# Attention and two feed-forwards on one core: the feed-forwards without GpSimd, weights in order of deadline

## The chip, the cores and the metric

The kernel runs on one core of a Trainium2 chip. The metric is the device time of one execution in microseconds (us); lower is better. Engines are called TensorE (PE in the rows, its weight loads PEld), VectorE (DVE), ScalarE (ACT), GpSimd (POOL) and SyncE (SP, which issues all DMAs here).

## The reference

```python
def reference(q, k, v, moe_*, moe2_*):             # q, k, v: (4, 8, 576, 64)
    x = attention(rotate(q), rotate(k), v)           # softmax(q k^T / 8) v
    x = x.transpose(0, 2, 1, 3).reshape(2304, 512)
    h = x @ moe_w_in                                 # 512 x 2048
    g = np.where(h > 0, h, np.exp(np.minimum(h, 0)) - 1)
    x = g @ moe_w_out                                # 2048 x 512
    a, b = x @ moe2_w1, x @ moe2_w2                  # 512 x 1024 each
    return (a * b @ moe2_w3) @ moe2_w_out            # 1024 x 1024, 1024 x 512
```

All values are float32.

## The kernel before, in words

Every large product is made from two-part operands: a value is split into a high part (a copy rounded to the type that the matmul reads) and a rest (value minus high part, also rounded), and three matmuls (high by high, high by rest, rest by high, `PAIRS` of line 24) stand for one. A split is one copy (`copy_hi`, lines 81 to 87) and one subtraction (line 79). Operations on whole tiles are mostly 128 partitions by 512 columns.

**Weights.** They come from memory as 64-bit words (`fetch_w`, line 92). `weight_steps` (line 97) turns one 128x512 block into its two parts in six steps: `rebase` (ScalarE, line 110), `shift`, `low` and `sign` (VectorE, lines 113, 116, 119), `high` (ScalarE, line 124) and `rest` (line 128, on the engine handed in: GpSimd).

**Stage 1**, attention, runs to about 304 us. It also prepares the first six blocks of w_in and of w_out (`PF` = 6). It is not changed.

**Stage 2**, the first feed-forward (lines 535 to 695). Five token tiles, three of 512 and two of 384 columns (`TT`), by 16 blocks f of the hidden width make 80 steps, numbered n. `part_h` (line 566) does 12 matmuls for h; then relu and exp on ScalarE, e on VectorE (line 577), and g's split: the copy on ScalarE (line 83), the rest on VectorE (line 79). `part_y` (line 582) does 12 matmuls of g with w_out into four banks that collect over f. The list `behind` holds y back by `LAG` = 2 steps; g has `LAG` + 1 buffers. When a tile ends, all y that are still held back are done before the next tile's first h, and the next tile's x is split (`split_x`, line 548).

Blocks of weights become due in `todo_w` (line 666): w_in and w_out alternate by f, one and a half a step, the last at step 13. `ready_in_out` issues the first four steps behind the h of one step and leaves `high` and `rest` in the list `late`, which the next `part_h` empties between exp and e. From step 15 on, `EARLY` (line 49) names the steps in which the second feed-forward's weights are made: 24 blocks of w_out2 and w3 (`ready_early`, 4/3 a step over steps 15 to 32) are split, stored in memory (`keep`) and later read back (`again`); then 16 blocks of w1 and w2 (`ready_half`), of which each pair is combined on GpSimd into seven blocks of 256 columns, split on GpSimd and stored. A staging tile has two buffers and a raw block has two. In the last token tile w_out2 (`load_o`) and w3 (`load_3`) are read back into the slots of w_in and w_out whose last reader is done; these DMAs stand in SyncE's queue and wait there.

**Stage 3**, the second feed-forward (lines 698 to 871). First W = w3 w_out2 is made, 24 matmuls for each of eight blocks (`part_w`, line 711); between blocks the x of the first token pair is summed (`x_sums`, line 728, on GpSimd) and split (`x_split`). Then come 24 groups (`group`, line 816): seven products of 384 columns (`multiply`, line 769) from which VectorE and ScalarE make two gates (`gate`), and, one group later, 18 matmuls of the gates with W (`part_o`, line 786). When eight groups are done, six outputs are copied out of their banks into a buffer of four (`ev`) and stored.

Each engine works through its instructions in their order. In stage 2 that order is written out by hand, step by step:

```python
part_h(ti, f, x[ti])
behind.append((ti, f))
if len(behind) > LAG:
    part_y(*behind.pop(0))
while todo_w and todo_w[0][0] <= n:
    ...
```

Of the kernel before, what the change touches and what calls it, by code (L numbers as in the profile page):

```python
# [18 lines left out]
P = 128  # L19
# [27 lines left out]
NA = 2 * PF  # L47

EARLY = (*(15 + 3 * i // 4 for i in range(24)), *(n for f in range(8) for n in (33 + 5 * f, 34 + 5 * f)))

LOAD_O = (0, 1, 1, 2, 3, 3, 4, 5)
LAG, LOAD_3, DEEP, W_AT = 2, 6, 2, NA
# [8 lines left out]
def kernel(  # L61
# [468 lines left out]
    def load_3(i):  # L530
        for z in range(2):
            w3_t[i, z] = slot(8 + 2 * (i % DEEP) + z, F32R, [P, 2, 512], "w")
            again(w3_t[i, z], ("3", i, z))

    with ExitStack() as c2:
# [5 lines left out]
        g_p = pool2("g", LAG + 1)  # L541
# [22 lines left out]
        gs, ys, late = {}, {}, []  # L564

        def part_h(ti, f, x):
# [52 lines left out]
        halves = {}  # L619

        def ready_half(key):
# [11 lines left out]
            pool.tensor_tensor(t1, b12, b11, op=ALU.subtract)  # L633
            pool.tensor_tensor(t2, b22, t1, op=ALU.subtract)
            pool.tensor_tensor(b12, b22, b12, op=ALU.subtract)
            order = (b11, b21, t2, t1, b12, b21, b22)
            for y in range(0, 7, 2):
                blocks = order[y:y + 2]
                st = stage_p.tile([P, len(blocks), 2, 256], F32R, tag="stage", name="wab", padded_shape=[P, 2, 2, 256])
                for i, b in enumerate(blocks):  # L640
                    if y + i == 5:
                        pool.tensor_tensor(b, b, t2, op=ALU.subtract)
                    copy_hi(st[:, i, 0], b, pool)
                    pool.tensor_tensor(st[:, i, 1], b, st[:, i, 0].bitcast(F32), op=ALU.subtract)
                keep(("ab", f, y // 2), st)
# [15 lines left out]
        for i in range(DEEP):  # L661
# [271 lines left out]
```

## Time and profile before

| | |
|---|---|
| median of three runs | 1047.61 us (1044.87 to 1047.69) |
| the profiled execution | 1042.17 us, its span 1040.4 us |
| TensorE busy | 1011.4 us, 97% |
| VectorE busy | 626.8 us, 60% |
| ScalarE busy | 497.2 us, 48% |
| GpSimd busy | 424.8 us, 41% |
| VectorE by slices of 26 us, stage 2 | about 8 of 10 up to 490 us, about 5 of 10 after |
| granted TensorE clock, mean | 0.994 |

A row of the trace names the line, the engine, the operation and the tiles (result<-operands). "Busy" of TensorE holds matmuls whose ends are modelled, so a short wait may not show as a gap; how many matmuls a stretch holds shows it. An idle time in brackets is followed by what ended it.

### The profile page before, as it was taken

What the parts mean: (1) busy time and instruction counts of PE and PEld (TensorE: products, weight loads), DVE (VectorE), ACT (ScalarE), POOL (GpSimd) and SP (SyncE); (2) the same over time, 40 slices, a digit from 0 to 9 for tenths busy, and PEclk for the clock granted to TensorE, in tenths of its full rate; (3) what the DMA queues carried; (4) which work ended last, traced back from release to release, by engine and by line L of the source; (5) the groups of instructions that cost most, each with busy time, mean ns of one, the idle gap of its engine ahead of it and who ended that gap; (6) DMA issues with size and microseconds to landing.
All of it is one profiled execution on the core that took longest, in us unless ns stands there. A gap on an engine that the chain in (4) does not pass through costs nothing.

```text
span 1040.4 us, 15562 instructions
## 1 busy us (share of the span) xinstructions
PE 1011.4 (97%) x5660; PEld 862.8 (83%) x5660; DVE 626.8 (60%) x1006; ACT 497.2 (48%) x1012; POOL 424.8 (41%) x465
## 2 busy tenths in 40 slices
PE   8999999999999989998999999999999999999997
PEld 7777777777768768876888999999899899999996
DVE  5698989888748888787534555532333444434323
ACT  3677777777645656555533444443223232222222
POOL 3789888888303332322544365560500211300000
PEclk9999999999999999999999999999999999999999
DMA  5988787876661005677332233466464446555511
GB/s 175 255 232 243 220 241 217 241 220 184 205 257 68 1 1 175 249 242 244 122 124 102 93 148 139 188 240 223 162 218 159 160 164 215 158 162 209 172 66 61
DMA packets 63101, 180.86 MB, mean 174 GB/s; under 512 B 7984, under 2 KB 9648, under 8 KB 63024
## 3 DMA queue, kind: packets, MB, share of 16 engines
q1 hardware_dynamic: 63024, 179.86, 53.2%
q8 instruction: 45, 0.74, 0.3%
q14 instruction: 32, 0.26, 0.1%
HBM read 121.31 MB, written 31.98 MB: 147 GB/s over the span
## 4 chain that ended last, share of the span: by engine, by line
PE 66%; issue 12%; DVE 11%; ACT 4%; POOL 3%; DMA 3%; SPq 0%; ACTq 0%; POOLq 0%; DVEq 0%
PE h L561 11%; PE y L589 11%; PE A L774 9%; PE o L800 9%; PE B L774 7%; PE w L716 4%; POOL w L128 3%; PE o L402 3%; PE s L286 3%; DVE nm L298 3%; PE ptp L334 3%; DMA kept<-w 2%; PE s L278 2%; DVE wr L116 2%; ACT pr L302 1%
## 5 line engine op out<-in xcount | busy, mean ns | idle before, releaser
L589 PE MATMUL y<-g,w 128*128 128x512 f32 (+1 forms) x960 | 213.3, 371 | 8.0 <-ACT g L83 4.0
L561 PE MATMUL h<-xt,w 128*128 128x512 f32 (+1 forms) x960 | 211.7, 369 | 5.4 <-ACT w L124 2.6
L589 PEld LDWEIGHTS y<-g,w 128*128 128x128 f32 x960 | 175.4, 189 | 35.2 <-DVE g L79 7.6
L561 PEld LDWEIGHTS h<-xt,w 128*128 128x128 f32 x960 | 174.2, 188 | 32.3 <-ACT w L124 3.4
L302 ACT ACTIVATE pr<-s,nm 128x576 f32<-128x576 f32 x144 | 106.6, 740 | 61.3 <-DVE nm L298 60.1
L128 POOL TENSOR_TENSOR w<-wr,w 128x512 fp32r<-128x512 f32 x56 | 74.2, 1330 | 147.2 <-ACT w L124 126.5
L298 DVE TENSOR_REDUCE nm<-s 128x1 f32<-128x576 f32 x144 | 107.0, 750 | 19.9 <-PE s L278 13.1
L774 PE MATMUL A<-xc,set 128*128 128x384 f32 x576 | 116.1, 336 | 0.9 <-ACT p L826 0.8
L79 DVE TENSOR_TENSOR g<-e,g 128x512 fp32r<-128x512 f32 (+1 forms) x80 | 81.4, 1018 | 58.4 <-ACT g L83 48.6
L800 PE MATMUL o<-W,g 128*128 128x512 f32 x432 | 111.6, 394 | 0.4 <-DVE g L784 0.2
L774 PEld LDWEIGHTS A<-xc,set 128*128 128x128 f32 x576 | 102.4, 188 | 8.6 <-ACT p L826 2.2
L577 DVE SCALAR_TENSOR_TENSOR e<-e,h 128x512 f32<-128x512 f32 (+1 forms) x80 | 50.4, 630 | 74.7 <-ACT e L573 74.7
L286 PE MATMUL s<-st 128*128 128x288 f32 x480 | 93.1, 316 | 1.6 <-ACT pr L302 1.4
L800 PEld LDWEIGHTS o<-W,g 128*128 128x128 f32 x432 | 79.9, 188 | 13.7 <-DVE g L784 0.7
L334 PE MATMUL ptp<-idt,pr 128*128 128x128 f32 x576 | 91.0, 281 | 0.0
L83 ACT ACTIVATE g<-p 128x384 fp32r<-128x384 f32 x48 | 25.2, 526 | 134.3 <-DVE p L846 96.0
L334 PEld LDWEIGHTS ptp<-idt,pr 128*128 128x128 f32 x576 | 65.9, 143 | 27.8 <-issue 12.6
L774 PE MATMUL B<-xc,set 128*128 128x384 f32 x432 | 86.5, 334 | 0.0
L182 POOL TENSOR_TENSOR raw_qk<-raw_qk,tab 128x640 f32<-128x640 f32 (+1 forms) x56 | 83.2, 1486 | 2.2
L838 DVE TENSOR_TENSOR p<-A,p 128x384 f32<-128x384 f32 x24 | 13.4, 558 | 110.5 <-PE A L774 110.5
L572 ACT ACTIVATE e<-h 128x512 f32<-128x512 f32 (+1 forms) x80 | 43.8, 547 | 73.0 <-PE h L561 71.0
L774 PEld LDWEIGHTS B<-xc,set 128*128 128x128 f32 x432 | 76.0, 188 | 0.0
(323 smaller groups left out, 1480.9 us busy)
## 6 DMA issues: line engine op xcount, KB each, us to landing
set<-kept SPq DMA_DIRECT2D x72, 512.0 KB, 3.8
st<-hl SPq DMA_DIRECT2D x180, 144.0 KB, 2.5
raw<-w_ SPq DMA_DIRECT2D x32, 512.0 KB, 3.8
kept<-w SPq DMA_DIRECT2D x24, 512.0 KB, 3.3
kept<-wab SPq DMA_DIRECT2D x24, 512.0 KB, 2.6
w<-kept SPq DMA_DIRECT2D x24, 512.0 KB, 4.2
raw_qk<-k_ SPq DMA_DIRECT2D x15, 640.0 KB, 4.3
raw_qk<-q_ SPq DMA_DIRECT2D x15, 576.0 KB, 4.3
```

The costliest lines, as they stand in the source:

```text
L79: lo_eng.tensor_tensor(lo, src, hi.bitcast(F32), op=ALU.subtract)
L128: rest_eng.tensor_tensor(made[0][:, 1], r, made[0][:, 0].bitcast(F32), op=ALU.subtract)
L182: pool.tensor_tensor(r[:, z], r[:, z], tab[:, w, z, TAB[w]], op=ALU.mult)
L286: pe.matmul(s[:, n, :288], st[:, j, 0, c * P:c * P + P], st[:, j, z, n * 288:(n + 1) * 288], start=(z == 1), stop=(z == 2),)
L298: dve.tensor_reduce(nm, s[:, :, :288], axis=AX.XY, op=ALU.max, negate=True)
L302: act.activation(pr_t[u, c][:, j].rearrange("p (n i) -> p n i", n=2), s[:, :, :288], ACTF.Exp, bias=nm, accum_out=sums_t[u, hf][:, at_:at_ ...
L334: pe.transpose(pt[:, kc], pr[:, at_:at_ + P], idt)
L561: pe.matmul(ps[:, :n], w[:, a, cc * P:(cc + 1) * P], x[cc][:, c], start=(i == 0), stop=(i == 11))
L577: dve.scalar_tensor_tensor(g, e, -1.0, ps[:, :n], op0=ALU.add, op1=ALU.max)
L589: pe.matmul(ys[ti][o][:, :n], wout[f][:, a, o * P:(o + 1) * P], g[:, c], start=(f == 0 and i == 0), stop=(f == NF - 1 and i == 2),)
L774: pe.matmul(ps[:, :HB], w[:, a, c * P:(c + 1) * P], x[:, c, b], start=(start and i == 0), stop=i == 5, skip_group_check=True,)
L800: pe.matmul(outs[p, o], g[:, a, o % 3 * P:o % 3 * P + P], wW[f][:, c], start=(f == 0 and i == 0), stop=(f == NG - 1 and i == 2),)
```

## The change

- The rests of all weights (line 128) in the first feed-forward, the combining and splitting of w1 and w2, and the sums of x in the second, go from GpSimd to VectorE. The copies in the splits of w1 and w2 go to ScalarE.
- What a weight leaves for the next step is held in two lists. ScalarE's part (`late_act`) is issued after exp as before, VectorE's (`late_dve`) between e and g's rest.
- The seven blocks of a pair of w1 and w2 are made in four parts, one a step (`ready_part`).
- Weights of the first feed-forward are fetched and made in the order of the step that first reads them, 4/3 a step from step 0. The early weights are made one a step from step 17, and none in the first or the last step of a tile.
- `LAG` is 3; g keeps three buffers.
- Five blocks of w3 are read back in the last token tile (before: two), and the loads of the first two sets come between the blocks of W. x is summed and split ahead of each block of W.
- In a group the sums of x for the next pair follow the first add. In the last group the product that feeds the first gate comes before the one that feeds the second, and the last 18 matmuls run in order of their output.

```diff
-EARLY = (*(15 + 3 * i // 4 for i in range(24)), *(n for f in range(8) for n in (33 + 5 * f, 34 + 5 * f)))
+STEP = [n for n in range(17, 80) if n % 16 not in (15, 0)]
+EARLY = (*STEP[:24], *(n for f in range(8) for n in STEP[23 + 4 * f:25 + 4 * f]))
-LAG, LOAD_3, DEEP, W_AT = 2, 6, 2, NA
+LAG, LOAD_3, SLOT_3, W_AT = 3, (6, 7, 11, 12, 13), (8, 10, 14, 16, 18, 8, 10, 8), NA
...
-            w3_t[i, z] = slot(8 + 2 * (i % DEEP) + z, F32R, [P, 2, 512], "w")
+            w3_t[i, z] = slot(SLOT_3[i] + z, F32R, [P, 2, 512], "w")
...
-        g_p = pool2("g", LAG + 1)
+        g_p = pool2("g", 3)
...
             act.activation(e, e, ACTF.Exp, scale=-1.0)
-            while late:
-                late.pop(0)()
+            run(late_act)
             g = e
             dve.scalar_tensor_tensor(g, e, -1.0, ps[:, :n], op0=ALU.add, op1=ALU.max)
+            run(late_dve)
             t = g_p.tile([P, 2, n], F32R, tag="g", name="g", padded_shape=[P, 2, 512])
             split(t, g, act, dve)
...
-            steps = weight_steps(i, raws.pop(i), lambda t: (win, wout)[i % 2].__setitem__(i // 2, t), pool)
+            steps = weight_steps(i, raws.pop(i), lambda t: (win, wout)[i % 2].__setitem__(i // 2, t), dve)
             for step in steps[:4]:
                 step()
-            late.extend(steps[4:])
+            late_act.append(steps[4])
+            late_dve.append(steps[5])
...
-            steps = weight_steps(None, raws.pop(key), lambda t: done.__setitem__(0, t), pool)
+            steps = weight_steps(None, raws.pop(key), lambda t: done.__setitem__(0, t), dve)
...
-            late.extend((*steps[4:], lambda: keep(key, done[0])))
+            late_act.append(steps[4])
+            late_dve.extend((steps[5], lambda: keep(key, done[0])))
...
+        def ready_part():
+
+            if not parts:
+                return
+            f, y, blocks = parts.pop(0)
+            made = []
+            if y == 2:
+                dve.tensor_tensor(blocks[1], blocks[1], t2_of[f], op=ALU.subtract)
+
+            def high():
+                made.append(stage_p.tile(
+                    [P, len(blocks), 2, 256], F32R, tag="stage", name="wab", padded_shape=[P, 2, 2, 256]
+                ))
                 for i, b in enumerate(blocks):
+                    copy_hi(made[0][:, i, 0], b, act)
+
+            def rest():
+                for i, b in enumerate(blocks):
+                    dve.tensor_tensor(made[0][:, i, 1], b, made[0][:, i, 0].bitcast(F32), op=ALU.subtract)
+                keep(("ab", f, y), made[0])
+
+            late_act.append(high)
+            late_dve.append(rest)
...
-        todo_w = [(1 + 2 * w // 3, NA + w) for w in range(2 * NF - NA)]
+        todo_w = sorted(range(NA, 2 * NF), key=lambda i: (i // 2 + LAG * (i % 2), i))
+        fetch = list(todo_w)
+        todo_w = [(3 * w // 4, i) for w, i in enumerate(todo_w)]
...
+            last = n + 1 == N3
+            if last:
+                c12()
+                lows = g0(), c22()
+                for low in lows:
+                    low()
+                return
...
             for i in range(7):
-                part_w(i)
-                if i + DEEP < 8:
-                    load_3(i + DEEP)
+                if i in (2, 4):
+                    load_set(i // 2 - 1)
                 x_sums(0, i)
                 x_split(0, i)
+                part_w(i)
+                if i in (0, 1, 5):
+                    load_3({0: 5, 1: 6, 5: 7}[i])
...
-            part_o(N3 - 1, (3, 4, 5, 0, 1, 2))
+            part_o(N3 - 1, range(6))
```

## Rows read from the trace of the kernel before

**Rows 1.** Chain of waits in order of time: start us, us, what.

```profile
500.04 2.72 PE y L589 x12
...
707.71 6.24 PE y L589 x36
```

**Rows 2.** Timeline of TensorE: start us, us, instructions merged [idle before <-releaser].

```profile
304.42 2.11 PE L561 MATMUL h<-xt,w 128*128 128x512 f32 x8
...
308.01 0.49 PE L589 MATMUL y<-g,w 128*128 128x512 f32 x1 [1.48 <-ACT g L83]
...
382.83 0.73 PE L561 MATMUL h<-xt,w 128*128 128x512 f32 x2 [2.10 <-ACT w L124]
...
485.81 0.49 PE L589 MATMUL y<-g,w 128*128 128x512 f32 x1 [2.27 <-ACT g L83]
```

**Rows 3.** Busy us by stretches of 20 us; (x) counts instructions, PEclk is granted clock.

```profile
core 0: us, PE busy (x) PEld busy (x) DVE busy (x) ACT busy (x) POOL busy (x), PEclk, DMA share, GB/s
...
320.00:340.00 20.00, 20.00 (x90) 16.58 (x89) 16.97 (x23) 12.26 (x22) 7.27 (x6) 1.00 0.00 0
...
360.00:380.00 20.00, 18.01 (x76) 13.56 (x75) 16.90 (x22) 12.14 (x21) 7.95 (x6) 1.00 0.00 0
380.00:400.00 20.00, 17.08 (x73) 13.10 (x72) 15.23 (x24) 11.32 (x21) 2.75 (x2) 1.00 0.17 54
...
480.00:500.00 20.00, 15.81 (x60) 12.40 (x61) 14.75 (x23) 11.65 (x20) 4.08 (x4) 0.91 0.57 203
...
640.00:660.00 20.00, 19.23 (x106) 18.01 (x105) 14.16 (x21) 10.73 (x22) 10.98 (x16) 1.00 0.32 116
660.00:680.00 20.00, 20.00 (x118) 20.00 (x117) 10.52 (x16) 8.23 (x17) 12.17 (x16) 1.00 0.75 293
```

**Rows 4.** VectorE by line and shape, 310 to 385 us: count | busy us, mean ns | idle before.

```profile
L119 DVE SCALAR_TENSOR_TENSOR wr<-raw,wr 128x512 int32<-128x512 int32 x20 | 20.6, 1032 | 0.7
L79 DVE TENSOR_TENSOR g<-e,g 128x512 fp32r<-128x512 f32 x13 | 16.2, 1244 | 9.1 <-ACT g L83 9.1
L116 DVE SCALAR_TENSOR_TENSOR wr<-raw,wr 128x512 int32<-128x512 int32 x20 | 13.9, 693 | 0.7
L577 DVE SCALAR_TENSOR_TENSOR e<-e,h 128x512 f32<-128x512 f32 x13 | 8.8, 677 | 0.0
L113 DVE TENSOR_SCALAR wr<-wr 128x512 int32<-128x512 int32 x20 | 8.3, 416 | 0.0
```

**Rows 5.** Timeline of VectorE and GpSimd between 366 and 392 us.

```profile
371.71 1.67 DVE L119 SCALAR_TENSOR_TENSOR wr<-raw,wr 128x512 int32<-128x512 int32 x1
...
389.65 0.69 DVE L79 TENSOR_TENSOR g<-e,g 128x512 fp32r<-128x512 f32 x1 [0.70 <-PE y L589]
...
371.36 1.47 POOL L128 TENSOR_TENSOR w<-wr,w 128x512 fp32r<-128x512 f32 x1 [3.09 <-ACT w L124]
```

**Rows 6.** Timeline of ScalarE at the end of the second token tile.

```profile
473.74 0.63 ACT L124 ACTIVATE w<-wr 128x512 fp32r<-128x512 f32 x1 [3.05 <-DMA kept<-w]
...
481.83 0.68 ACT L110 ACTIVATE wr<-raw 128x512 f32<-128x512 f32 x1 [1.92 <-DMA raw<-w_]
```

**Rows 7.** Waits (who <- whom: us in total, times, longest) and VectorE's timeline, stage 3.

```profile
DVE p L838 <- PE A L774: 110.5, 24, 6.8
...
PE A L774 <- ACT p L826: 0.8, 2, 0.4
...
812.45 1.36 DVE L851 TENSOR_TENSOR p<-u,p 128x384 f32<-128x384 f32 x1
```

**Rows 8.** Timeline of TensorE and ScalarE at the end of the program.

```profile
1030.55 0.72 PE L800 MATMUL o<-W,g 128*128 128x512 f32 x2 [0.16 <-ACT g L83]
1031.50 3.92 PE L800 MATMUL o<-W,g 128*128 128x512 f32 x16 [0.23 <-DVE g L784]
...
1036.52 0.60 ACT L809 ACTIVATE ev<-o 128x512 f32<-128x512 f32 x1 [1.82 <-DMA out_<-ev]
```

**Rows 9.** SyncE's own waits; and DMA issues (count, KB each, us to landing).

```profile
SPq L524 <- PE h L561: 11.9, 1, 11.9
...
raw<-w_ SPq DMA_DIRECT2D x32, 512.0 KB, 3.8
```

More of the change, by code (lines that the diff above doesn't have):

```diff
@@ L562, in project, with run @@
                     i += 1
-        gs, ys, late = {}, {}, []
+        gs, ys, late_act, late_dve = {}, {}, [], []
+        def run(late):
+            while late:
+                late.pop(0)()
         def part_h(ti, f, x):
@@ L632, in ready_half @@
             t1, t2 = t[:, :256], t[:, 256:]
[L633 to L639, printed above, removed]
-                for i, b in enumerate(blocks):
[L641 to L645, printed above, removed]
+            dve.tensor_tensor(t1, b12, b11, op=ALU.subtract)
+            dve.tensor_tensor(t2, b22, t1, op=ALU.subtract)
+            dve.tensor_tensor(b12, b22, b12, op=ALU.subtract)
+            parts.extend((f, y, blocks) for y, blocks in enumerate(((b11, b21), (t2, t1), (b12, b21), (b22,))))
+            t2_of[f] = t2
+        def ready_part():
[9 more added lines that the diff above has]
+                ))
+                for i, b in enumerate(blocks):
+                    copy_hi(made[0][:, i, 0], b, act)
[5 more added lines that the diff above has]
+            late_dve.append(rest)
         ahead = [(ready_early, ("o", j, 0), w_o2[j]) for j in range(8)]
@@ L692 @@
                     task(i)
+            run(late_act)
+            run(late_dve)
             for s_ in behind:
                 part_y(*s_)
-        assert not ahead and not tasks
+        assert not ahead and not tasks and not parts
     with ExitStack() as c3:
@@ L821, in group @@
             more = p + 1 < NPAIR
-            if more and f and f != 6:
-                x_sums(p + 1, {7: 6}.get(f, f - 1))
             multiply(A, x[0], w[0], True)
@@ L828, in group @@
             dve.tensor_tensor(p1, B_[:, :HB], p1, op=ALU.add)
+            if more and f and f != 6:
+                x_sums(p + 1, {7: 6}.get(f, f - 1))
             part_o(n - 1, (3, 4))
@@ L843, in group, with c22, c12, g0 @@
                 x_split(p + 1, {7: 6}.get(f, f - 1))
[L844 to L852 removed]
+            def c22():
+                multiply(A, x[5], w[5], False)
+                if last:
+                    part_o(n - 1, (1, 2))
+                dve.tensor_tensor(p5, A[:, :HB], p5, op=ALU.mult)
+                return gate(n, 1, p5)
+            def c12():
+                multiply(B_, x[6], w[6], False)
+                dve.tensor_tensor(u2, B_[:, :HB], u2, op=ALU.add)
+            def g0():
+                dve.tensor_tensor(p1, u2, p1, op=ALU.mult)
+                return gate(n, 0, p1)
+            last = n + 1 == N3
+            if last:
+                c12()
[3 more added lines that the diff above has]
+                return
+            part_o(n - 1, (1, 2))
+            low = c22()
+            c12()
+            low()
+            g0()()
         N3 = NPAIR * NG
         with tc.manual_schedule():
[L856 to L857 removed]
             for i in range(7):
[L859 to L861 removed]
+                if i in (2, 4):
+                    load_set(i // 2 - 1)
                 x_sums(0, i)
                 x_split(0, i)
+                part_w(i)
+                if i in (0, 1, 5):
+                    load_3({0: 5, 1: 6, 5: 7}[i])
             for n in range(N3):
```

35 lines of the change are left out of this document (13 added, 22 removed).

## The prediction

> **What bounds the kernel now.** I read the page's first two parts first: TensorE is busy 97% of the span, so only its gaps and its end can be won. Busy hides gaps, because a matmul's end is modelled; so I then read the chain of waits for an undisturbed pace and counted matmuls against it. In the first feed-forward twelve matmuls of 512 columns take 2.72 us and 36 of 384 columns 6.24 us [rows 1], that is 0.2267 and 0.1733 us each, and 5.44 us for a step of 512 columns (12 h, 12 y). The code has 48 steps of 512 and 32 of 384 columns. When TensorE resumes h at 304.42 [rows 2], 28 of the h matmuls are done (counted in its timeline); the last y ends at 707.71 + 6.24 = 713.95 [rows 1]. Left at 304.42: 1152 - 28 = 1124 x 0.2267 = 254.8 us, and 768 x 0.1733 = 133.1 us, together 387.9 us. It takes 713.95 - 304.42 = 409.5 us. **21.6 us of stall** lie in the first feed-forward, and the table by stretch says where [rows 3]: an undisturbed 20 us hold 90 matmuls of 512 columns or 118 of 384; the stretches from 360 and 380 hold 76 and 73, that from 480 holds 60, that from 640 holds 106. So: the first token tile while weights are still made (up to 400), the end of the second tile (from 480, where the granted clock also fell to a mean of 0.91, so to 1.2 instead of 2.4 GHz for a part of the stretch, around a wait of TensorE of over 2 us [rows 2, 3]), the last tile boundary (645), and 1.5 us idle at the first y [rows 2].
>
> Why they are there: the VectorE rows of the first tile [rows 4]. Per step there are e (677 ns), g's rest (1244 ns, with 9.1 / 13 = 0.70 us of idling before each, for ScalarE's copy of g), and 1.5 weights of 416 + 693 + 1032 ns. That is 0.68 + 0.70 + 1.24 + 1.5 x 2.14 = 5.83 us against TensorE's 5.44: **VectorE's queue is the bound of the first tile**, and weights and g come late by the difference until TensorE waits for them (2.10 us at 382.83, 2.27 us at 485.81) [rows 2]. Two of the three long durations aren't VectorE's own: a sign step takes 1.67 us beside a GpSimd instruction, and g's rest 0.69 us at the end of the tile, when GpSimd is idle [rows 5]. In the second tile ScalarE's queue is also held by DMAs: 3.05 us for a staging buffer still being stored, 1.92 us for a raw weight [rows 6].
>
> **The change part by part.**
>
> Weights' rests from GpSimd to VectorE. Adds 44 instructions of 128x512 with two SBUF inputs (20 weights here, 24 early ones); the nearest row is g's rest alone, 0.69 us [rows 5], so 30 us of VectorE time over two and a half tiles. Removes the stretching: sign from 1.03 to 0.69, g's rest from 1.24 to 0.69. The rests stand between e and g's rest, which fills the 0.70 us idle. With 20 weights over 15 steps (4/3 a step), a step costs 0.68 + 0.69 + 4/3 x (0.42 + 0.69 + 0.69 + 0.69) = **4.69 us, below TensorE's 5.44**. Bounds of a rest: 0.69 (alone) to 1.30 (GpSimd's own time for it is 1.3 to 1.5 [rows 5]); I take 0.69, the same operation on the same engine. Even at 1.1 the step stays under 5.44.
>
> The Trainium skill's page "SBUF — State Buffer", section "Who interferes with whom", says that a VectorE instruction with two SBUF inputs contends with a GpSimd instruction that reads SBUF, and that one of them then waits for the whole of the other. The trace agrees: e, whose second input is in PSUM, stays at 677 ns in the same stretch where the two-input operations stretch [rows 4]. By that rule no stretch is left in the feed-forwards, as in my sum.
>
> y three steps behind h. Moves 12 matmuls of y per step, adds none. g's allowance from h's end to its use grows from 2 x 5.44 = 10.9 to 16.3 us. But g keeps three buffers, so ScalarE's copy of g(n) now waits for y(n-3), which ends 2.72 us after h(n) does. Queued behind it on ScalarE are the rebase of the next weights and the next step's relu; on VectorE g's rest. Copy and 4/3 rebases of some 0.63 to 0.68 us [rows 6] end at 2.72 + 0.63 + 0.9 = 4.25 us, before the next h ends at 5.44: I take zero; if that cover fails it costs at most the 2.72 a step, which the longer allowance has twice. At a tile's end four y (10.9 us) rather than three stand ahead of the next tile's first h; the x splits (two copies and four rests, at most 6 x 0.69 = 4.1 us of VectorE) follow g's rest at about 4 us and end near 8.2. The boundary stalls go, also because no weight is begun in the last or first step of a tile.
>
> Weights by deadline, early ones at one a step. The order gives each w_in at least three steps (16 us); its chain is about 4 us. One early weight a step in place of 4/3 leaves two steps (10.9 us) from one raw weight to the next use of its buffer: four operations of about 3 us, and 3.8 us for the DMA [rows 9]. Margin about 4 us, so the ScalarE waits of [rows 6] go.
>
> w1/w2 blocks: per f, 11 VectorE operations of 128x256 and seven ScalarE copies, spread over four steps. At the price of 512 columns they are 7.6 us at most, with the two weights' 2 x 1.8 and four times e and g's rest (4 x 1.37) 16.7 us, against 4 x 4.16 = 16.6 of TensorE; half the columns must cost less, so it fits, and the longer allowance covers an uneven step.
>
> What is late next: the start. With two weights begun at step 0, y(1)'s rest is ready at about 315.1 when wanted at 314.7; 0.4 us, and I leave 1 us for all of the feed-forward. **Sum there: -20.6 us.**
>
> Loads of w3, sets and x sums at the head of the second feed-forward: TensorE has no gap there before, so nothing to win. x sums on VectorE are 14 operations, at most 14 x 0.69 = 9.7 us over 7 x 24 x 0.2267 = 38 us of part_w. In the groups at most six (4.1 us) now stand ahead of the add of line 838, which waits 110.5 / 24 = 4.6 us for TensorE today [rows 7]: zero. With GpSimd goes the stretched product of line 851 (1.36 us) behind which line 826 came late twice, with TensorE idle 0.4 us each time [rows 7]; the cadence around it lost some 0.6 us each: **-1.2 us** (-0.8 by the idle alone).
>
> Last group reordered: the first gate's product now has 6 x 0.2267 = 1.4 us of matmuls of o, and another product, between itself and the last o, so they start at once. Today the 18 matmuls run from 1030.55 to 1031.50 + 3.92 = 1035.42 [rows 8], 4.87 us for 18 x 0.2267 = 4.1; and the last output copy waits 1.82 us for a store to free a buffer [rows 8]. Earlier first copies start the stores earlier. I take **-1.8 us** (bounds -0.8, the gap alone, and -2.6, all of both).
>
> Sum: -20.6 - 1.2 - 1.8 = -23.6 us: 1042.17 (profiled execution, span 1040.4) to 1018.6. The median of the runs is 1047.61, 5.4 us above that execution; I know no reason in the rows, so I take the difference from the median: **1024 us**.
>
> **The rivals.**
>
> A. VectorE stays the bound of the first tiles, because its order (wait for ScalarE's copy, then rests, then weights) costs what the stretching did. Against it: the idle 0.70 us has a rest to fill it. Then the first two tiles keep about half of their 18 us (21.6 less the start's 1.5 and the 2.0 at 645): 1033.
>
> B. The other side: a full queue is given more work. If the stretching doesn't come from GpSimd but from VectorE's own succession of operations, the first tile's step costs 0.68 + 0.70 + 1.24 + 4/3 x (2.14 + 0.69) = 6.4 us; over 16 steps (6.4 - 5.83) x 16 = 9 us more, over the early weights' 24 steps some 3 more, less the one extra step of lag (5.44) and the end's 1.8: 1047.6 + 5 = 1053. It decides from a g rest above about 1.2 us with GpSimd idle; the row at 389.65 (0.69) speaks against it [rows 5]. The Trainium skill ("Perfetto Trace Analysis", "Optimizing Scalar/DVE Operations") advises the reverse of this change, moving work off a saturated VectorE, GpSimd included, though it adds that between these two it might not help. Here the row on the stretching decides for the second half of that sentence.
>
> C. The sync queue. In the last tile the loads of w_o and w3 wait in it for a y that now comes one step (4.16 us) later, with raw weights and stores behind them; today one such wait is 11.9 us [rows 9]. Each raw weight is fetched four steps ahead there, which covers one blocked step or two; if not, ScalarE stands behind a rebase for up to two steps: +8, 1032.
>
> **How the numbers follow.** Forecast (1024, own range 1018 to 1029) 0.72; A or C or a mix 0.17; no net change (gains eaten by a new wait) 0.04; B 0.07. The low end is the profiled execution less the whole of 21.6, 1.2 and 2.6: 1042.2 - 25.4 = 1016.8, taken 1017; the high end takes in A: 1035. A measurement of this kernel can tell about 0.3% (3 us) from no change. Faster 0.89, same 0.04, slower 0.07.
>
> **What would show it.** In the changed profile: GpSimd without instructions after 300 us; g's rest and the sign step at 0.69 us throughout; 88 to 90 matmuls in each 20 us of the first three tiles and some 388.5 us from the resumed h to the last y; VectorE between 80% and 90% busy in the first tile; no wait of line 774 for line 826; the last o matmuls without a gap. A g rest still above 1 us, or ScalarE waiting over 2 us for y or for a DMA with TensorE waiting behind, would make it wrong.

## The result, and the profile after

| | before | after |
|---|---|---|
| median of four runs each, us (lowest to highest) | 1046.24 (1043.32 to 1047.69) | **1018.45** (1017.7 to 1019.9) |
| after / before, 95% interval | | **0.9739** [0.9713, 0.9766] |
| profiled execution, us; its span | 1042.17; 1040.4 | 1017.7; 1015.8 |
| mean granted clock over the span | 0.994 | 0.997 |

The forecast, 1024 us, had the sign and the size: 27.8 us are won by the medians and 24.6 us between the two profiled spans, where the sum gave 23.6; the median lies near the low end of the forecast's range. The page of after begins so (busy us, share of the span, instructions of each engine; of the 40 slices only GpSimd's are shown):

```profile
PE 1001.6 (99%) x5660; PEld 863.0 (85%) x5660; DVE 657.9 (65%) x1180; ACT 516.8 (51%) x1068; POOL 223.2 (22%) x235
...
POOL 3788898888500000000000000000000000000000
```

TensorE has gone from 97% to 99%, and GpSimd has no instruction after its eleventh slice (279 us). The stretches of [rows 3], now of after, in the same columns:

```profile
320.00:340.00 20.00, 20.00 (x90) 16.57 (x89) 19.29 (x33) 14.47 (x25) 0.00 (x0) 1.00 0.00 0
340.00:360.00 20.00, 20.00 (x90) 16.57 (x89) 19.32 (x34) 15.09 (x27) 0.00 (x0) 1.00 0.00 1
360.00:380.00 20.00, 20.00 (x90) 16.57 (x89) 17.64 (x30) 13.19 (x22) 0.00 (x0) 1.00 0.00 1
380.00:400.00 20.00, 20.00 (x89) 16.54 (x89) 10.20 (x17) 10.72 (x18) 0.00 (x0) 1.00 0.13 43
480.00:500.00 20.00, 20.00 (x90) 16.55 (x89) 16.90 (x29) 13.14 (x23) 0.00 (x0) 1.00 0.63 211
640.00:660.00 20.00, 20.00 (x118) 20.00 (x117) 14.31 (x32) 9.90 (x23) 0.00 (x0) 1.00 0.99 356
```

Each stretch holds the undisturbed count, 89 or 90 matmuls or 118, at a granted clock of 1.00 (2.4 GHz), where before had 76, 73, 60 and 106. VectorE is *fuller* than before from 320 to 360 us, 96 to 97% against the 85% of [rows 3] and the 87% of the row below, and TensorE waits for nothing. The second stretch of before:

```profile
340.00:360.00 20.00, 19.67 (x87) 15.80 (x86) 17.42 (x24) 12.86 (x23) 6.37 (x6) 1.00 0.00 1
```

VectorE's rows by line and shape in after, 310 to 385 us, answer to [rows 4] (count | busy us, mean ns | idle before):

```profile
L120 DVE SCALAR_TENSOR_TENSOR wr<-raw,wr 128x512 int32<-128x512 int32 x20 | 13.8, 692 | 0.7
L129 DVE TENSOR_TENSOR w<-wr,w 128x512 fp32r<-128x512 f32 x20 | 13.4, 689 | 0.9
L117 DVE SCALAR_TENSOR_TENSOR wr<-raw,wr 128x512 int32<-128x512 int32 x19 | 13.1, 692 | 0.6
L80 DVE TENSOR_TENSOR g<-e,g 128x512 fp32r<-128x512 f32 x15 | 10.3, 690 | 0.9 <-ACT g L84 0.8
L581 DVE SCALAR_TENSOR_TENSOR e<-e,h 128x512 f32<-128x512 f32 x15 | 10.2, 681 | 0.9 <-ACT e L578 0.9
L114 DVE TENSOR_SCALAR wr<-wr 128x512 int32<-128x512 int32 x19 | 8.0, 421 | 0.0
```

The sign step (line 120) has gone from 1032 to 692 ns, g's rest (line 80) from 1244 to 690, and VectorE idles 0.9 us in all before it (0.8 of it for ScalarE's copy) instead of 9.1. The 20 rests of weights (line 129) are new in this queue and cost 689 ns each.

For the experiments I cut the span by TensorE's timeline: a tile of the first feed-forward is taken from its first h to the next tile's (the fifth to the first product of W); **FF1** goes from the resumed h (304.42 and 304.58 us) to the first product of W; **groups** from there to the last 18 o matmuls; then these 18, and what follows the last matmul. Stage 1, which no edit touches, ends anywhere from 303.5 to 307.3 us, so experiments are compared by these columns more than by totals. **Clock** sums 20 us x (1 - granted clock) over the stretches of 20 us from 300 to 1000 us: the most that the lower level (1.2 GHz) can have cost, less where TensorE waited in them anyway. The last column is the median of the timed runs, for e5 and e9 the one run taken.

| kernel, us | tile 1 | tile 2 | tile 3 | tile 4 | tile 5 | FF1 | groups | 18 o | tail | clock | time |
|---|---|---|---|---|---|---|---|---|---|---|---|
| before | 101.3 | 96.8 | 87.1 | 67.0 | 68.0 | 409.4 | 316.75 | 4.88 | 4.94 | 1.8 | 1046.24 |
| after | 91.7 | 87.0 | 87.1 | 66.6 | 66.5 | 388.1 | 314.73 | 4.25 | 4.05 | 0 | 1018.45 |
| e1, y two steps behind | 95.5 | 87.1 | 87.0 | 66.6 | 66.5 | 392.0 | 314.70 | 4.25 | 4.04 | 1.8 | 1021.81 |
| e2, GpSimd back | 97.2 | 87.0 | 87.1 | 66.6 | 66.5 | 393.6 | 316.39 | 4.25 | 4.36 | 0 | 1026.6 |
| e3, old order and pace | 94.7 | 91.0 | 87.1 | 66.6 | 66.5 | 395.2 | 314.68 | 4.25 | 4.05 | 1.8 | 1025.43 |
| e4, before, engines alone | 107.6 | 106.1 | 90.6 | 77.3 | 76.7 | 447.6 | 325.09 | 4.88 | 4.93 | 13.8 | 1091.59 |
| e5, GpSimd beside VectorE | 103.8 | 87.0 | 87.1 | 66.5 | 66.6 | 400.3 | 314.68 | 4.25 | 4.04 | 5.2 | 1032.38 |
| e6, old end | 91.7 | 87.1 | 87.0 | 66.6 | 66.6 | 388.2 | 315.02 | 4.88 | 4.95 | 0 | 1020.2 |
| e8, rests done three times | 114.5 | 87.0 | 87.0 | 66.6 | 66.6 | 411.0 | 314.73 | 4.25 | 4.04 | 5.0 | 1040.68 |
| e9, before again | 101.3 | 96.7 | 87.2 | 67.2 | 68.0 | 409.6 | 316.69 | 4.90 | 4.91 | 1.8 | 1042.23 |
| e10, before against itself | 103.7 | 97.6 | 87.3 | 66.7 | 67.9 | 412.4 | 316.71 | 4.90 | 4.90 | 6.8 | 1045.38 |
| e11, rests ahead of e | 105.0 | 87.0 | 87.1 | 66.5 | 66.9 | 401.8 | 314.68 | 4.25 | 4.04 | 3.4 | 1032.22 |
| e12, blocks in one step | 91.7 | 87.1 | 87.0 | 80.9 | 74.0 | 410.0 | 314.70 | 4.25 | 4.04 | 6.8 | 1038.54 |
| e13, x sums first | 91.7 | 87.1 | 87.0 | 66.6 | 66.5 | 388.2 | 323.0 | 4.25 | 4.04 | 1.8 | 1025.68 |

Between before and after the two profiled executions differ by 21.3 us in FF1, 2.0 in the groups, 0.63 in the 18 o and 0.89 in the tail. Within FF1, after leaves 0.2 us over the 387.9 that the matmuls themselves take.

### The profile page after: what moved, and what is told of

The parts are those of the page before. It is cut to its first block, busy times and chain, and to the rows that moved or that the text cites. A ratio compares the mean times of both kernels' runs of the same rounds, so it can differ in the third digit from the quotient of the medians.

```text
span 1015.8 us, 15512 instructions
## 1 busy us (share of the span) xinstructions
PE 1001.6 (99%) x5660; PEld 863.0 (85%) x5660; DVE 657.9 (65%) x1180; ACT 516.8 (51%) x1068; POOL 223.2 (22%) x235
## 4 chain that ended last, share of the span: by engine, by line
PE 85%; DVE 8%; issue 3%; ACT 2%; DMA 1%; ACTq 0%; DVEq 0%
PE h L562 19%; PE y L594 19%; PE A L802 10%; PE o L828 10%; PE B L802 7%; PE w L744 4%; PE o L403 4%; PE s L287 3%; DVE nm L299 3%; PE ptp L335 3%; PE s L279 2%; DVE wr L117 1%; ACT pr L303 1%; PE warm L479 1%; DVE ri L358 1%
## 5 line engine op out<-in xcount | busy, mean ns | idle before, releaser
L562 PE MATMUL h<-xt,w 128*128 128x512 f32 (+1 forms) x960 | 208.5, 368 | 0.0
L594 PE MATMUL y<-g,w 128*128 128x512 f32 (+1 forms) x960 | 207.7, 367 | 0.0
L866 DVE TENSOR_TENSOR p<-A,p 128x384 f32<-128x384 f32 x24 | 13.4, 558 | 98.3 <-PE A L802 98.3
L84 ACT ACTIVATE g<-e 128x512 fp32r<-128x512 f32 (+1 forms) x80 | 47.1, 589 | 49.9 <-DVE e L581 25.2
L287 PEld LDWEIGHTS s<-st 128*128 128x128 f32 x480 | 67.5, 189 | 5.5 <-ACT pr L303 5.0
```

The lines of the kernel that those rows point to most:

```text
L84: act.activation(hi, src, ACTF.Copy, scale=scale)
L287: pe.matmul(s[:, n, :288], st[:, j, 0, c * P:c * P + P], st[:, j, z, n * 288:(n + 1) * 288], start=(z == 1), stop=(z == 2),)
L562: pe.matmul(ps[:, :n], w[:, a, cc * P:(cc + 1) * P], x[cc][:, c], start=(i == 0), stop=(i == 11))
L594: pe.matmul(ys[ti][o][:, :n], wout[f][:, a, o * P:(o + 1) * P], g[:, c], start=(f == 0 and i == 0), stop=(f == NF - 1 and i == 2),)
```

## The experiments

Three questions were open. Does the stretching on VectorE come from GpSimd (my theory) or from VectorE's own succession (rival B)? Which part of the change carries the gain? How much room has VectorE now, that is, was "the step stays under TensorE's" a comfortable margin?

### GpSimd brought back, and GpSimd set beside VectorE (e2, e5)

e2 gives the subtractions back to GpSimd and keeps order, pace and lag of the change, and the places in the queues:

```
- steps = weight_steps(i, ..., dve)      + steps = weight_steps(i, ..., pool)
- dve.tensor_tensor(t1, b12, b11, ...)   + pool.tensor_tensor(t1, b12, b11, ...)
  ... so for the early weights, the blocks' subtractions and the x sums
```

> The changed kernel with GpSimd back: the weights' rests, the subtractions of the w1 and w2 blocks and the sums of x run on GpSimd; order, pace and lag stay those of the change (the copies of the w1 and w2 blocks stay on ScalarE). Theory (the engine matters through the stretching of VectorE): rest of g and sign go back to 1.0 to 1.3 us and the 0.70 us idle returns, so a step of the first tile costs 0.68 + 0.70 + 1.24 + 4/3 x 2.14 = 5.47 us against 5.44; with the longer lag that hardly shows: 0 to 4 us in the first feed-forward, 1 to 2 us in the groups, total 1019 to 1024. Rival (without the engine's change nothing is won): 10 us or more of the stalls come back, total 1030 or above.

Measured: 1026.6 us, 0.9813 [0.9779, 0.9846] of before. Tile 1 is 5.5 us longer than after's, the groups 1.66, the tail 0.3, nothing else. VectorE by line, 310 to 385 us:

```profile
L120 DVE SCALAR_TENSOR_TENSOR wr<-raw,wr 128x512 int32<-128x512 int32 x19 | 18.0, 947 | 0.6
...
L80 DVE TENSOR_TENSOR g<-e,g 128x512 fp32r<-128x512 f32 x14 | 17.4, 1240 | 10.5 <-ACT g L84 10.5
```

The long durations are back with GpSimd, and so is the idling ahead of g's rest. Tile 1 loses a little more than I expected, the groups what I expected, and the total lies above the 1019 to 1024 of the theory and below the rival's 1030. Three quarters of FF1's gain stay (5.5 of 21.3 us are lost): with the new order, pace, lag and places, the old engines and the stretching cost only these 5.5 us there.

e5 keeps after as it is and lets GpSimd do, beside each of the 20 weights, two subtractions of 256 columns into a scratch tile that nobody reads:

```
+ def both():
+     for z in range(2): pool.tensor_tensor(scratch, xT[...], <half of the high part>, op=subtract)
+     steps[5]()
- late_dve.append(steps[5])
+ late_dve.append(both)
```

> The changed kernel, in which GpSimd also does a subtraction with two operands in SBUF, in two halves of 256 columns into a scratch tile, behind each high copy of the first feed-forward's 20 weights; VectorE's own work is unchanged. Theory (the stretching of VectorE comes from GpSimd): VectorE's instructions with two SBUF operands (sign, low, both rests) that run beside a GpSimd instruction take 1.0 to 1.7 us instead of 0.69, e with one operand in PSUM stays at 0.68; a mean above 0.8 us for the rests. Rival (the stretching came from VectorE's own succession of operations): all stay at 0.69.

Measured: 1032.38 us (one run). VectorE and then GpSimd, 310 to 395 us:

```profile
L80 DVE TENSOR_TENSOR g<-e,g 128x512 fp32r<-128x512 f32 x16 | 18.7, 1168 | 0.8 <-ACT g L84 0.8
L129 DVE TENSOR_TENSOR w<-wr,w 128x512 fp32r<-128x512 f32 x20 | 16.1, 822 | 1.0
L120 DVE SCALAR_TENSOR_TENSOR wr<-raw,wr 128x512 int32<-128x512 int32 x20 | 15.9, 796 | 0.7
...
L114 DVE TENSOR_SCALAR wr<-wr 128x512 int32<-128x512 int32 x20 | 13.2, 660 | 0.0
L582 DVE SCALAR_TENSOR_TENSOR e<-e,h 128x512 f32<-128x512 f32 x15 | 10.2, 679 | 0.0
```

```profile
L617 POOL TENSOR_TENSOR scratch<-xT,w 128x256 f32<-128x256 f32 x39 | 41.4, 1060 | 54.7 <-ACT w L125 53.2
```

VectorE does the same instructions as in after, and with GpSimd busy beside it g's rest goes from 690 to 1168 ns, the weights' rest from 689 to 822, the sign step from 692 to 796, the shift (line 114) from 421 to 660; e, which reads PSUM, stays at 679. The low step, which I expected to stretch too, stays at 693; the last section says why such means differ. So the stretching is GpSimd's doing and rival B's premise falls. The added VectorE time is 16 x 0.478 + 20 x (0.133 + 0.104 + 0.239) = 17.2 us, and tile 1 grows by 12.1, of which up to 5.2 are the lower clock that followed TensorE's waits: 5 to 10 us found room. The Trainium skill's page "SBUF — State Buffer", section "Who interferes with whom", says that a VectorE instruction with two SBUF inputs contends with a GpSimd instruction that reads SBUF, and that one with a single SBUF input doesn't unless it runs in a two-port mode. The trace agrees for the rests and the sign step (two SBUF inputs, stretched) and for e (one, not stretched); the shift reads one SBUF operand and is stretched too, and no row says in which mode it runs.

### How much room VectorE has (e8)

Each rest of the 20 weights is done three times in place; the result is the same, and 20 x 2 x 0.69 = 27.6 us are added to VectorE's queue in tile 1:

```
- late_dve.append(steps[5])
+ late_dve.extend((steps[5],) * 3)
```

> The changed kernel with the rest of each of the 20 weights of the first feed-forward done three times on VectorE (same result). Theory (VectorE's queue bounds the first tile as soon as a step of it passes TensorE's 5.44 us): a step costs 0.68 + 0.69 + 4/3 x (1.80 + 3 x 0.69) = 6.5 us, 16 us late after 15 steps, of which the allowance of g hides about 12: 3 to 8 us of stall before 400 us, none after; total 1021 to 1026. Rival (there is room to spare on VectorE): no stall.

Measured: 1040.68 us, 0.9947 [0.9931, 0.9964] of before. Tile 1 grows by 22.8 us, where I expected 3 to 8: the room is 27.6 - 22.8 = 4.8 us, or up to 9.8 if all of the clock's 5.0 is taken off the growth, as in e5. Two stretches and three rows of TensorE's timeline:

```profile
340.00:360.00 20.00, 17.25 (x77) 13.96 (x76) 19.22 (x32) 10.65 (x20) 0.00 (x0) 1.00 0.00 1
...
380.00:400.00 20.00, 13.51 (x49) 10.43 (x50) 19.26 (x32) 10.58 (x18) 0.00 (x0) 0.83 0.00 1
```

```profile
317.73 4.37 PE L594 MATMUL y<-g,w 128*128 128x512 f32 x11 [2.71 <-DVE g L80]
...
373.16 2.58 PE L562 MATMUL h<-xt,w 128*128 128x512 f32 x10 [2.58 <-DVE w L129]
...
388.74 0.73 PE L562 MATMUL h<-xt,w 128*128 128x512 f32 x2 [3.00 <-ACT w L125]
```

VectorE shows the same 19.2 of 20 us as in after, so it is the bound now; TensorE does 77 and 49 matmuls instead of 90 and 89. Of its idle times in tile 1, 10.0 us are h waiting for a weight (four waits), which a longer lag of y doesn't cover, and 7.0 us are y waiting for g's rest (four waits), in spite of the third step of lag. I expected g's allowance to hide about 12 us; with VectorE's own slack, 5 to 10 found room in all, and why y still waits isn't shown. So after stands close to the edge: nothing waits at 96%, and 5 to 10 us more in a tile of 87 do make it wait.

Where my 4.69 us a step went wrong is in after's rows above: nearly all of the 20 weights' steps lie within 75 us, 13.8 steps of 5.44, since the first h of the tile run without a y between them. That is 1.45 weights a step, not 1.33, and the six lines with the x split (2.6 + 0.8 us) make 72.2 us in 75, **5.2 us a step**. At 1.1 us a rest it would have been 5.8: "even at 1.1" was wrong.

### The engines alone, from before (e4)

Only the engines of the change, in the kernel before: rests, subtractions and x sums from GpSimd to VectorE and the blocks' high copies to ScalarE, at the places where GpSimd had them:

```
- steps = weight_steps(i, ..., pool)         + steps = weight_steps(i, ..., dve)
- copy_hi(st[:, i, 0], b, pool)              + copy_hi(st[:, i, 0], b, act)
- pool.tensor_tensor(st[:, i, 1], b, ...)    + dve.tensor_tensor(st[:, i, 1], b, ...)
  ... so for t1, t2, b12 and the x sums
```

> The kernel before with only the engines changed: rests, w1 and w2 subtractions and x sums on VectorE, the w1 and w2 copies on ScalarE, all at the places in the order that they had; lag 2, old pace, old end. Theory (a rest costs VectorE 0.69 us and gives back less than that where the 0.70 us idle isn't filled): 0.68 + 0.70 + 0.69 + 3/2 x 2.49 = 5.81 us a step against 5.83 before, so the first feed-forward keeps 15 to 22 us of stall; 1 to 2 us are won in the groups; total 1038 to 1046. Rival (GpSimd's contention alone was the cause): 12 us or more are won, total below 1034.

Measured: 1091.59 us, **1.0434** [1.0395, 1.0474]: *slower* than before by 45 us where I expected 0 to 8 us less time. All five tiles and the groups lose. TensorE, ScalarE and VectorE, a row of each timeline:

```profile
619.96 4.48 PE L589 MATMUL y<-g,w 128*128 128x384 f32 x12 [4.50 <-ACT g L83]
```

```profile
615.87 0.42 ACT L83 ACTIVATE wab<-wr 128x256 fp32r<-128x256 f32 x1 [3.01 <-DMA kept<-wab]
```

```profile
347.66 0.69 DVE L128 TENSOR_TENSOR w<-wr,w 128x512 fp32r<-128x512 f32 x1 [0.70 <-ACT w L124]
```

Nothing is stretched here (0.69), yet a rest now stands in VectorE's queue behind ScalarE's high copy and *ahead of* the next e: 0.70 us of idling in the queue that everyone needs, where GpSimd waited alone. ScalarE's copies of the blocks, seven in one step, wait 3.01 us for a store (and 2.25 and 0.82 us for VectorE's subtractions of the same blocks); relu, exp and the copy of g stand behind them, and TensorE waits 4.50 us for g. Part of the loss is TensorE's clock, at most 13.8 - 1.8 = 12 us of the 45. e4 was a miss of mine, and the next three runs ask where these 45 us lie, each by undoing one place in the kernel after.

### The places, one by one (e11, e12, e13)

e11 puts the rests ahead of e again:

```
+ run(late_dve)
  dve.scalar_tensor_tensor(g, e, -1.0, ps[:, :n], op0=ALU.add, op1=ALU.max)
- run(late_dve)
```

> The changed kernel with one thing moved: the rests of the weights stand ahead of e on VectorE instead of between e and g's rest. Theory (VectorE's order counts: ahead of e a rest waits 0.70 us for the high copy, and the idle before g's rest comes back): as in the run with only the engines changed, a step with one weight costs 5.16 us and one with two 6.96, on average 5.76 against 5.44 at 4/3 a step; the first tile has only some 5 us of room (the run with thrice the rests kept 22.8 of 27.7 us), so it grows by 6 to 12 us; one weight a step in the second tile fits. Total 1024 to 1031. Rival (only the sum of VectorE's work counts): 0 to 2 us.

Measured: 1032.22 us, 0.9868 [0.985, 0.9885] of before; tile 1 grows by 13.3 us, a little more than expected, up to 3.4 of it by the clock. One stretch, and two rows of VectorE and one of TensorE:

```profile
340.00:360.00 20.00, 19.41 (x85) 15.49 (x84) 15.23 (x26) 10.90 (x19) 0.00 (x0) 1.00 0.01 1
```

```profile
359.20 0.69 DVE L129 TENSOR_TENSOR w<-wr,w 128x512 fp32r<-128x512 f32 x1 [0.70 <-ACT w L125]
...
361.25 0.69 DVE L80 TENSOR_TENSOR g<-e,g 128x512 fp32r<-128x512 f32 x1 [0.76 <-ACT g L84]
```

```profile
381.92 1.22 PE L562 MATMUL h<-xt,w 128*128 128x512 f32 x2 [4.45 <-ACT w L125]
```

VectorE is busy for 15.2 us of 20, not 19.3, and yet it is the bound: in a step with one weight it waits twice for ScalarE, 0.70 and 0.76 us. Put between e and g's rest, the same instruction waits for nothing and fills the second wait (in after, 0.9 us of idling in all before 15 g rests). Placing work in a wait that its engine has anyway is called weaving below.

e12 makes all blocks of w1 and w2 in the step in which their inputs are ready, instead of over four:

```
  (in ready_half, behind t2_of)
+ while parts:
+     ready_part(); run(late_act); run(late_dve)
```

> The changed kernel with the seven blocks of a pair of w1 and w2 made, split and stored in the step in which the second weight is ready, as before the change, but on VectorE and ScalarE; lag 3. Theory (with only two staging buffers, ScalarE waits some 3 us for the stores in the middle of a pair, and h's relu stands behind it; on GpSimd that wait held up nobody): in the run with only the engines changed the last three tiles lost 24 us; the longer lag hides a part: 5 to 18 us more in tiles three to five, total 1023 to 1036. Rival (the lag hides all of it): within 2 us.

Measured: 1038.54 us, 0.9926 [0.9905, 0.9947] of before; tiles 4 and 5 grow by 14.3 and 7.5 us, tile 3 by nothing, 21.8 in all, more than expected, up to 6.8 of it by the clock. ScalarE, then TensorE:

```profile
629.89 0.72 ACT L84 ACTIVATE wab<-wr 128x256 fp32r<-128x256 f32 x2 [3.01 <-DMA kept<-wab]
...
631.48 0.47 ACT L577 ACTIVATE e<-h 128x384 f32<-128x384 f32 x1
```

```profile
633.76 2.56 PE L594 MATMUL y<-g,w 128*128 128x384 f32 x6 [5.64 <-ACT g L84]
```

It is the wait of e4 again: the copies of one step fill the staging buffers, ScalarE stands 3.01 us for a store, the relu at 631.48 comes late and TensorE idles 5.64 us. The same pair also holds ScalarE 2.25 us for VectorE's subtraction and 0.55 us for a second store, so the store alone isn't the whole delay. In after a ScalarE copy waits for the store too (9.0 us in 5 waits, below), and no TensorE wait follows.

e13 puts the x sums of the next part at the head of a group, ahead of the add that TensorE's next product waits for:

```
  (in group)
+ if more and f and f != 6: x_sums(p + 1, ...)
  ... the work of the group
- if more and f and f != 6: x_sums(p + 1, ...)
```

> The changed kernel with the sums of x at the head of the group, ahead of the first add, on VectorE. Theory (up to six sums, 3.3 us, then delay the add that frees the bank of the fourth product): 7 to 9 us more in the groups, as in the run with only the engines changed (+8.4), nothing elsewhere; total 1025 to 1028. Rival (the order in the group doesn't matter): within 1 us.

Measured: 1025.68 us, 0.9807 [0.9783, 0.9831] of before; the groups grow by 8.3 us, as expected. VectorE and TensorE:

```profile
818.64 0.55 DVE L767 TENSOR_TENSOR s<-xT 128x384 f32<-128x384 f32 x1
...
821.96 0.55 DVE L856 TENSOR_TENSOR p<-B,p 128x384 f32<-128x384 f32 x1
```

```profile
822.56 1.95 PE L802 MATMUL B<-xc,set 128*128 128x384 f32 x6 [2.00 <-DVE p L856]
```

Six sums of 0.55 us are the 3.3 us between the two VectorE rows; TensorE waits 2.00 us for the add behind them.

### Lag, order, end (e1, e3, e6)

e1 lets y follow two steps behind h: `LAG ... = 3` becomes `2`. The order of the weights is computed from `LAG`, so each w_out also comes due one step earlier in that order.

> The changed kernel with y two steps behind h instead of three; g keeps three buffers. Theory (VectorE's shorter queue is what removed the stalls, the lag only covers the start and the tile ends): the 1.5 to 2.2 us at the first y come back, and at each of the four tile ends y of the last step wants g 5.44 us after its h when it is ready at about 4.1, so 0 to 1 us each. First feed-forward (resumed h to last y) 390.5 to 393 us against 388.3 in the changed kernel; total 1020 to 1023. Rival (the longer lag is what hides a queue that is still late): most of the stalls come back, 400 us and more, total 1030 or above.

Measured: 1021.81 us, 0.9771 [0.9739, 0.9802] of before. Tile 1 grows by 3.8 us and nothing else changes: the wait at the first y comes back as expected, the tile ends show none. TensorE in e1, then the same y in before, and a stretch of e1 behind it:

```profile
307.37 0.51 PE L594 MATMUL y<-g,w 128*128 128x512 f32 x1 [1.48 <-ACT g L84]
308.09 4.06 PE L594 MATMUL y<-g,w 128*128 128x512 f32 x11 [0.22 <-DVE g L80]
```

```profile
308.73 2.79 PE L589 MATMUL y<-g,w 128*128 128x512 f32 x11 [0.23 <-DVE g L79]
```

```profile
310.00:312.00 2.00, 2.00 (x7) 1.54 (x6) 1.93 (x4) 0.84 (x2) 0.00 (x0) 0.50 1.02 406
```

1.48 and 0.22 us are, to 0.01, the idle times of before at its first y (1.48 [rows 2] and 0.23); a third step of lag removes just these. Up to 1.8 us of the rest is the clock: 0.50, the lower level, in the two microseconds shown, and eleven matmuls take 4.06 us where before has 2.79 for them after the same waits. From 318 us to the end of the tile TensorE has no wait at all: at its steady pace and at the tile's end two steps would do.

e3 takes back the order and the pace of the weights:

```
- EARLY = (*STEP[:24], ...)
+ EARLY = (*(15 + 3 * i // 4 for i in range(24)), ...)
- todo_w = sorted(range(NA, 2 * NF), key=lambda i: (i // 2 + LAG * (i % 2), i))
+ todo_w = list(range(NA, 2 * NF))
- todo_w = [(3 * w // 4, i) for w, i in enumerate(todo_w)]
+ todo_w = [(1 + 2 * w // 3, i) for w, i in enumerate(todo_w)]
```

> The changed kernel with the pace and order of before: w_in and w_out alternating, 3/2 a step from step 1, early weights 4/3 a step from step 15, also in the first and last steps of a tile. Theory (VectorE at 0.68 + 0.69 + 3/2 x 2.49 = 5.1 us a step stays under 5.44): no stall in the first tile beyond 1 us; in the second tile ScalarE waits for DMAs again and the tile ends carry weight steps, which the lag covers in part: 0 to 4 us, total 1018 to 1022. Rival (the order by deadline and the free tile ends are what removed the stalls): 6 us or more at 380 and 480 us, total 1025 or above.

Measured: 1025.43 us, 0.9803 [0.977, 0.9836] of before. Tile 1 grows by 3.0 us (TensorE waits 0.9 and 1.6 us for weights at 372 to 376 us) and tile 2 by 4.0 (g 1.3 and 0.6 us late at 473 to 476, and up to 1.8 us of clock behind it). Together 7 us, where I expected 0 to 4: what came is the rival's 6 us or more and its total above 1025, so order and pace matter more than my theory had it. The run doesn't part the order by deadline from the pace.

e6 takes back the order of the last group: `last = False`, and `part_o(N3 - 1, (3, 4, 5, 0, 1, 2))`.

> The changed kernel with the last group and the last 18 matmuls in the order of before. Theory: only the end changes; the last o matmuls wait about 0.7 us for the gates and the last output copies for stores: span longer by 1.5 to 2 us, total about 1020. Rival (the end was hidden behind the stores anyway): within 0.5 us.

Measured: 1020.2 us, 0.9758 [0.9714, 0.9802] of before. The last group grows by 0.29 us, the 18 o by 0.63, the tail by 0.90: 1.8, as expected.

### Before against itself (e9, e10)

The kernel before, unchanged, once more by itself and then timed: why is its median some 4 us above its profiled execution?

> The kernel before, once more, to see whether its stalls differ between executions (its runs differ by 4 us, those of the changed kernel by 2). Theory: stage 1, the products and the end take the same time, and the difference lies in the first two token tiles, where GpSimd and VectorE meet by chance: 20 to 26 us of stall there. Rival: the time differs everywhere by the same share (a clock).

> The kernel before, timed against itself, to see span and clock of several of its executions. Theory (its stalls of over 2 us let the granted clock fall in some executions longer than in others): the longer executions have the lower mean clock, and the difference of 3 to 5 us between them goes with it. Rival: the clock is the same in all.

Measured: e9 1042.23 us, with the columns of before, so it couldn't tell where longer executions lose; e10 1045.38 us (1041.35 to 1048.49 in 10 runs), ratio 1.0 [0.9982, 1.0019]. The profiled execution of e10 has a span of 1043.4 us, 3.0 more than the one of [rows 1 to 9]. Two of its stretches, and TensorE at the end of its first tile, say where:

```profile
380.00:400.00 20.00, 17.59 (x64) 13.47 (x63) 14.74 (x23) 9.59 (x17) 2.73 (x2) 0.83 0.18 54
...
480.00:500.00 20.00, 15.77 (x55) 11.50 (x54) 13.97 (x22) 11.07 (x19) 3.88 (x3) 0.83 0.60 197
```

```profile
382.88 1.22 PE L561 MATMUL h<-xt,w 128*128 128x512 f32 x2 [2.10 <-ACT w L124]
384.42 4.63 PE L561 MATMUL h<-xt,w 128*128 128x512 f32 x10 [0.31 <-POOL w L128]
```

The wait is that of [rows 2], 2.10 us for the same weight; but the two matmuls behind it take 1.22 us where [rows 2] show 0.73, and in the whole stretch TensorE does 64 where [rows 3] have 73, at a granted clock of 0.83 against 1.00. From 480 it does 55 for 60, at 0.83 against 0.91. (9 + 5) x 0.2267 = 3.2 us, about the difference; by the columns, tile 1 is 2.4 us longer and tile 2 0.8. A wait of some 2 us is followed by the lower level in one execution and not in another. Over 23 executions of before, spans go from 1039.4 to 1046.7 us and mean granted clocks from 0.997 to 0.985, with a correlation of -0.76: the longer ones have the lower clock, as e10's theory had it.

## Why the prediction was right, and where it wasn't

**The bound.** Right. 21.6 us of stall were counted in FF1, 20.6 were forecast to go, and 21.3 went. The first tile was bound by VectorE's queue, and the cause of its long instructions was GpSimd (e5). ScalarE's waits for DMAs in the second tile [rows 6] went as forecast: 13 waits, 23.6 us, in before and none in after. How much they mattered is less clear: in e3 ten of them, 22.4 us, are back and tile 2 loses 4.0 us. Of tile 2's 9.8 us no other run from after brings back any, so what removed the other 5.8 isn't shown.

**VectorE's step.** The price of an instruction was right (0.69 forecast, 0.689 to 0.692 measured), their number per step wasn't: 1.45 weights instead of 4/3, so 5.2 us instead of 4.69, and VectorE 96% busy where 80 to 90% were forecast. e8 and e5 leave 5 to 10 us of room in the tile, and the sentence on 1.1 us a rest falls. The forecast was saved by the price, not by the margin.

**Which part earns it.** The sum credits the engines: stretching gone, idle filled. Taken alone, the engines cost 45 us (e4). What the prediction named in passing, that the rests stand between e and g's rest, that the blocks are spread over four steps, that the sums come late in a group, is the condition on which moving the engines pays at all: 13.3, 21.8 and 8.3 us if undone (e11, e12, e13), each more than the 7.5 us of the columns that moving the engines wins in the end (after against e2). From the other side, the old engines with everything else of the change keep all but some 8 us of the gain (7.5 by the columns, 8.2 by the medians), so the stretching, which the sum makes the main term, didn't have to go for most of the gain. Order with pace is worth 7 (e3), lag 3.8 (e1), up to half of it by the clock that follows a wait. These shares don't add up to the whole; which part covers for which isn't shown.

**Lag and start.** The longer allowance was to cover the tile's end and uneven steps; e1 shows that in tile 1 it covers neither, since none is late there, and that its gain lies at the first y. y(1) was forecast 0.4 us late; its twelve matmuls take 0.1 us longer than y(0)'s, and the whole excess of FF1 over its matmuls is 0.2. TensorE's timeline of after:

```profile
309.24 2.88 PE L594 MATMUL y<-g,w 128*128 128x512 f32 x12
...
314.68 2.98 PE L594 MATMUL y<-g,w 128*128 128x512 f32 x12
```

The first y starts without the 1.48 us of [rows 2]. ScalarE's copy of g does wait for y(n-3), as worked out, and nobody behind it is late: of after's waits (who <- whom: us in total, times, longest) these three matter, and none of TensorE's for the feed-forwards is in the list.

```profile
DVE p L866 <- PE A L802: 98.3, 24, 6.8
...
ACT g L84 <- PE y L594: 23.9, 33, 0.9
...
ACT wab L84 <- DMA kept<-wab: 9.0, 5, 2.6
```

**Groups and end.** The groups gave 2.0 us for 1.2 forecast; the two waits of [rows 7] are gone, the add still waits 98.3 us for TensorE, so the sums are hidden. e2 gives 1.66 of the 2.0 to GpSimd's leaving and e6 0.29 to the new order of the last group. The end gave 0.63 + 0.89 = 1.5 for 1.8, and the last o run without a gap:

```profile
1006.06 5.64 PE L828 MATMUL o<-W,g 128*128 128x512 f32 x24
...
1011.92 0.69 DVE L835 COPY ev<-o 128x512 f32<-128x512 f32 x1 [0.85 <-DMA out_<-ev]
```

The last copy still waits for a store, 0.85 us instead of 1.82 [rows 8].

**The rivals.** A (order costs what the stretching did) is e11: 105.0 in tile 1 against before's 101.3, so it would have come had the rests been put elsewhere. B's premise is refuted by e5; yet a result on its side, 1091.59, is what e4 has, by another mechanism: queue order, not slow instructions. C wasn't seen: tiles 4 and 5 take 66.6 and 66.5 us, what their matmuls take.

**From the profiled execution to the median.** This step was mis-sized. "I know no reason in the rows, so I take the difference from the median" carried 5.4 us over to after. A hint was in the rows, in the 0.91 of [rows 3]: the 3.0 us that e10's profiled execution is longer lie behind TensorE's waits in tiles 1 and 2, at a lower clock, and without these waits the spread is smaller. After's four runs lie within 2.2 us where before's four lie within 4.4, and its median is 0.75 above its profiled execution. 1018.6 + 0.75 would have been 1019.4. So of the 5.5 us between the forecast and the median, 4.65 come from this step and 0.9 from the sum. That the clock accounts for all of before's spread isn't shown; the correlation leaves some of it open.

**Open.** How order by deadline, pace and the weight-free ends of a tile share e3's 7 us; how much of e4's 45 us is the lower clock (at most 12); what removed 5.8 of tile 2's 9.8 us.

## What to carry to other kernels

Work taken off a slow side engine paid here only where it landed in waits of the engine that got it: woven in, with order, pace and lag already changed, nearly the same instructions won some 8 us (after against e2); left in place in the kernel before, they lost 45. A wait in a side engine's queue, for a copy or for a store, stands in front of that engine's own work and of what needs it, not of the next relu or e; before moving the work, list those waits and see who will stand behind them. Count an engine's load over the stretch in which the work really lies (here 13.8 steps, not 15), and look behind which waits a spread between executions arises before you carry it over to a kernel without them.

## What the runs showed of the hardware that I had not expected

The means of [rows 4] mix two kinds, and who begins first decides which. Of before's 20 sign steps from 310 to 385 us, 13 took 0.69 us; the other 7, and 12 of the 13 g rests, began while a GpSimd rest ran, and each ended 0.54 to 0.56 us after that rest had ended, as in [rows 5], 371.71 + 1.67 against 371.36 + 1.47. The 7 low steps that began before the GpSimd rest they overlap kept 0.69, and these 7 GpSimd rests took 1.41 to 1.47 us, the others 1.28 to 1.30. So on either engine a two-input instruction came out longer when the other engine's was under way.

The shift (line 113 in before, 114 in after and e5), with one SBUF input, is stretched beside GpSimd as well: in e5 nine that overlap a GpSimd instruction take 0.94 to 0.97 us, the eleven others 0.41 to 0.42. It stayed at 0.416 in [rows 4] only because none of those 20 overlaps one; a later shift of before does, and takes 1.51 us. That shift, then two of e5:

```profile
401.81 1.51 DVE L113 TENSOR_SCALAR wr<-wr 128x512 int32<-128x512 int32 x1
```

```profile
343.96 0.96 DVE L114 TENSOR_SCALAR wr<-wr 128x512 int32<-128x512 int32 x1
...
346.29 0.42 DVE L114 TENSOR_SCALAR wr<-wr 128x512 int32<-128x512 int32 x1
```

And a wait of TensorE of 1.5 to 2.1 us is followed by the lower clock level in one execution and not in another (e1 against before, e10 against [rows 2, 3]), which costs about as much again as the wait: 2.0 us in e10's first tile.
